# A streaming joint kernel on one Trainium2 core: transform buffers, feature order and the place of the next batch's first products

## The chip, the cores and the metric

The kernel runs on one core of one Trainium2 chip. Times are device microseconds (us) of whole runs. Before the change the median of the three first runs was 272.15 us (272.11 to 273.55). The profile is of one run; its span, from the first to the last instruction, is some 1.8 us shorter than the run's time. PE is TensorE (matmul), DVE is VectorE, ACT is ScalarE, POOL is GpSimd.

## The reference

```python
B, T, D, K, U = 2, 4000, 512, 5, 8           # bf16 throughout
h = conv1d(x, w1, taps=5, same)              # sum over 5 taps of x[t+i] @ w1[i]
h = gelu(h)[:, ::2]                          # 2000 rows
f = gelu(conv1d(h, w2, taps=5, same))[:, ::2]  # 1000 rows
fe = f @ w_f ; ge = g @ w_g                  # (B,1000,512), (B,8,512)
j  = tanh(fe[:, :, None] + ge[:, None])      # (B,1000,8,512)
return j @ w_o                               # (B,1000,8,512)
```

The last product is by far the largest: 16,000 rows of 512. The kernel works on one batch as far as its joint product and then lays the second batch's convolutions between the joint tiles of the first.

## The kernel before: the parts that matter

Every operation is recorded with what it reads and writes and an estimated cost. A list scheduler then simulates the engines, picks on each engine the ready operation with the earliest "late" time, and writes out one fixed order for each engine. On PE, program order decides among what is ready.

```python
def simulate(self, pred, succ, late):
    ...
            now = [i for i in cand[e] if ready[i] <= t + 0.02]
            i = min(now) if e in ("pe", "sp") else min(now, key=lambda i: (late[i], i))
```

The strided convolutions use a fast algorithm ("Triple"): VectorE forms nine transformed inputs (s1, t1, sm, tm, t2, t0, s0, ti, si) from six input phases z(0) to z(5), and PE multiplies each with transformed weights. t1, tm, t0 and ti come from three fp32 intermediates q0, q1, q2.

```python
class Triple:
    HOME = {"t0": (0, 0), "ti": (0, 1), "t1": (0, 2), "tm": (0, 3),   # (0, i): own buffer
            "s1": (1, 0), "sm": (1, 1), "s0": (1, 3), "t2": (1, 4), "si": (1, 5)}  # (1, i): over z(i)
    def prepare(self, k0, k1, by_dma=False):        # channel blocks k0 to k1
        ...
            stt("dve", q(1, 0, E), z(0, 0, E), -2.0, z(2, 0, E))
            stt("dve", q(2, 0, E), z(2, 0, E), -2.0, z(4, 0, E))
            ...                                      # q0 from z(4), z(0)
        tt("dve", at("t2"), z(4), z(0), sub)
        tt("dve", at("s1"), z(1), z(3), add)         # overwrites z(0): behind q0, q1 and t2
        act(z(2), z(5, -1), ACT.Copy)
        tt("dve", at("si"), z(5), z(1), sub)
        tt("dve", at("sm"), z(3), z(1), sub)         # overwrites z(1)
        ...                                          # t1 = -q1 - q2
            tt("dve", at("t0"), q(2), q(0), sub)
            tt("dve", at("tm"), q(1), q(2), sub)
            tt("dve", at("ti"), q(0, 1), q(1), sub)
        tt("dve", at("s0"), z(2), z(3), sub)

def tail_zero(b, k0=0, k1=NK):                       # on GpSimd, before each prepare of conv2
    memset(hT[b][2:6, k0:k1, HOFF + NT3 - 1:HOFF + NT3])

def fe(b):                                           # features, thirds outside, channel blocks inside
    for i in (1, 0, 2):
        for m in range(NK):
            ...                                      # 4 matmuls into the next PSUM bank
            if (m + i) % 2: act(o, v, ACT.Copy)      # 6 copies
            else: ...tensor_copy on VectorE          # 6 copies

fe(0)
...                                                  # tanh of the first 1000 rows in three pieces
for i in range(2):
    first[i].prepare(0, 2); first[i].prepare(2, 4)   # first convolution of the next batch
    if i == 0: joint(6)                              # six joint tiles of 128 rows
    for m in range(NK): slot(first[i], m, (1, 0, 1, 0, 1))   # 9 products each, joint tiles between
```

## Time and profile before

| | before |
|---|---|
| time, median | 272.15 us |
| PE busy / span | 261.2 / 270.5 us |
| PE idle at start and end | 1.2 and 3.3 us |
| holes in PE that the change can reach | 1.9 + 1.5 + 0.7 + 0.6 us |

The page gives the busy time, share of the span and instruction count of each engine:

```profile
span 270.5 us, 4327 instructions
...
PE 261.2 (97%) x1582; PEld 152.4 (56%) x1582; DVE 199.4 (74%) x352; ACT 183.1 (68%) x306; POOL 7.5 (3%) x26
```

Its line of the chain that ended last, in shares of the span by engine, shows PE for over two thirds and VectorE next:

```profile
PE 69%; DVE 13%; issue 7%; ACT 5%; DMA 5%; POOL 0%; DVEq 0%; POOLq 0%
```

The view of PE's waits lists what PE waited for, the total, the number of times and the longest:

```profile
PE acc L417 <- DVE hT L404: 1.7, 1, 1.7
PE acc L417 <- DVE feT L973: 1.4, 1, 1.4
...
PE acc L417 <- ACT jT L409: 1.0, 2, 0.6
```

The windows view gives each engine's busy time in a stretch. From 57.7 to 90 us VectorE is full while PE has its holes; from 100 us on PE is full (the line of 100 to 121 us is shown; its timeline has no hole over 0.2 us after that):

```profile
57.70:80.50 22.80, 21.07 (x148) 14.16 (x147) 22.77 (x50) 12.21 (x27) 0.43 (x3) 1.00 1.11 198
80.50:90.00 9.50, 7.99 (x69) 5.36 (x68) 9.50 (x19) 5.61 (x12) 0.00 (x0) 1.00 0.20 35
...
100.00:121.00 21.00, 21.00 (x129) 12.52 (x128) 20.08 (x37) 18.50 (x36) 0.21 (x2) 1.00 0.27 89
```

The hole before the second convolution is best read from VectorE's timeline (start, duration, line, operation, out<-in, count, idle time before and its releaser):

```profile
57.73 1.35 DVE L585 SCALAR_TENSOR_TENSOR r32b<-hT 128x336 f32<-128x336 bf16 x3 [0.53 <-POOL hT L401]
58.99 0.33 DVE L404 TENSOR_TENSOR hT<-hT 128x334 bf16<-128x334 bf16 x1
59.23 0.50 DVE L740 SCALAR_TENSOR_TENSOR row<-r32b 128x334 bf16<-128x334 f32 x1
59.65 1.40 DVE L404 TENSOR_TENSOR hT<-hT 128x334 bf16<-128x334 bf16 x4
```

The zeroing by GpSimd releases VectorE at 57.73. Three q operations run first; then t2, t1 and, at 59.65, the group that begins with s1. PE has nothing to multiply until 60.03. The zeroing itself waits for ScalarE: it starts 0.06 us after the end of the gelu that writes this channel block, at 57.52.

PE's own timeline around the second group of holes:

```profile
89.53 0.74 PE L417 MATMUL acc<-zx,w_t 128*128 128x334 bf16 x4 [1.35 <-DVE feT L973]
90.11 0.73 PE L417 MATMUL acc<-row,w_t 128*128 128x334 bf16 x4
91.39 3.63 PE L417 MATMUL acc<-wo_sb,jT 128*128 128x512 bf16 x16 [0.56 <-ACT jT L409]
...
98.58 0.73 PE L417 MATMUL acc<-row,w_t 128*128 128x334 bf16 x4
99.76 1.04 PE L417 MATMUL acc<-wo_sb,jT 128*128 128x512 bf16 x4 [0.45 <-ACT jT L409]
```

A merged line covers several matmuls; a hole is the distance from the end of one group to the start of the next, taken start to start at 0.142 us per 334-column and 0.216 us per 512-column matmul. So the holes are 1.5 us before 89.53, 0.7 before 91.39 and 0.6 before 99.76. Holes quoted below are all computed this way; the bracketed wait is up to 0.2 us shorter (1.35, 0.56 and 0.45 here), because the record of a matmul runs on past the start of the next: that of the 334-column one at 79.77 is 0.30 us long, and the next starts at 79.91.

### The profile page before, as it was taken

The numbers are of one execution on the slowest core, as the hardware profiler recorded it, in microseconds if no ns is written. First come the engines' busy times: TensorE is split into PE (matmuls) and PEld (weight loads), VectorE is DVE, ScalarE is ACT, GpSimd is POOL, SyncE is SP. The second block draws the span as 40 slices with busy tenths as digits, with TensorE's granted clock in tenths as the row PEclk, the third lists the DMA queues.
The fourth block names the chain that finished last, engine by engine and source line by source line (L and its number), as shares of the span: only waits on it lengthen the run. The fifth ranks groups of instructions, "written<-read, shape, count | busy, mean of one in ns | idle before, by whom it ended". The sixth has DMA issues, their size and how long they took to land.

```text
span 270.5 us, 4327 instructions
## 1 busy us (share of the span) xinstructions
PE 261.2 (97%) x1582; PEld 152.4 (56%) x1582; DVE 199.4 (74%) x352; ACT 183.1 (68%) x306; POOL 7.5 (3%) x26
## 2 busy tenths in 40 slices
PE   8999999979999799999999999999999999999995
PEld 4987854436666345666655554555566444444442
DVE  0999999899999999993333799953424667656654
ACT  2787969784474999786366497574346995959720
POOL 1000005200000000000000000000000000000000
PEclk9999999999999999999999999999999999999999
DMA  7999988979992014111111121421110353454444
GB/s 248 312 191 210 330 191 144 170 147 201 185 199 39 16 42 156 41 59 58 59 41 58 48 91 40 158 78 58 61 58 1 103 171 116 159 192 156 147 147 133
DMA packets 56706, 33.91 MB, mean 125 GB/s; under 512 B 31582, under 2 KB 56430, under 8 KB 56686
## 3 DMA queue, kind: packets, MB, share of 16 engines
q1 hardware_dynamic: 54430, 31.49, 43.5%
q0 software_dynamic: 2112, 2.10, 4.5%
q8 instruction: 12, 0.20, 0.3%
q14 instruction: 8, 0.07, 0.1%
q10 hardware_dynamic: 144, 0.07, 0.1%
HBM read 7.86 MB, written 16.38 MB: 90 GB/s over the span
## 4 chain that ended last, share of the span: by engine, by line
PE 69%; DVE 13%; issue 7%; ACT 5%; DMA 5%; POOL 0%; DVEq 0%; POOLq 0%
PE acc L417 68%; ACT jT L409 4%; DMA half<-w_sb 3%; DMA half<-w_t 2%; DVE row L404 2%; DVE r L585 2%; DVE hT L404 1%; DVE r32b L585 1%; DVE row L740 1%; PE acc L510 1%; DVE row L585 1%; DVE feT L973 1%; DVE xt L404 1%; DVE r L404 1%; DVE zx L404 1%
## 5 line engine op out<-in xcount | busy, mean ns | idle before, releaser
L417 PE MATMUL acc<-wo_sb,jT 128*128 128x512 bf16 (+1 forms) x504 | 115.3, 377 | 1.0 <-ACT jT L409 1.0
L1020 DVE CAST ost<-acc 128x512 bf16<-128x512 f32 (+1 forms) x95 | 65.0, 688 | 32.2 <-PE acc L417 32.1
L409 ACT ACTIVATE jT<-feT,geT 128x1000 bf16<-128x1000 f32 (+16 forms) x100 | 75.4, 816 | 8.3 <-PE acc L417 8.2
L417 PEld LDWEIGHTS acc<-wo_sb,jT 128*128 128x128 bf16 x504 | 49.1, 98 | 53.8 <-ACT jT L409 1.9
L409 ACT ACTIVATE ost<-acc 128x512 bf16<-128x512 f32 (+1 forms) x31 | 18.0, 581 | 18.1 <-PE acc L417 16.9
L417 PE MATMUL acc<-row,w_sb 128*128 128x334 bf16 (+1 forms) x160 | 29.8, 305 | 0.0
L409 ACT ACTIVATE sd<-acc 128x334 f32<-128x334 f32 (+1 forms) x32 | 13.9, 445 | 16.2 <-PE acc L417 15.9
L417 PE MATMUL acc<-xt,w_sb 128*128 128x252 bf16 (+1 forms) x144 | 23.5, 305 | 0.0
L417 PEld LDWEIGHTS acc<-row,w_sb 128*128 128x128 bf16 x160 | 15.6, 97 | 8.3
L417 PE MATMUL acc<-hT,w_t 128*128 128x334 bf16 x96 | 17.7, 305 | 1.7 <-DVE hT L404 1.7
L409 ACT ACTIVATE hT<-acc 128x334 bf16<-128x334 f32 (+3 forms) x33 | 15.0, 461 | 4.8 <-PE acc L417 4.6
L417 PEld LDWEIGHTS acc<-xt,w_sb 128*128 128x128 bf16 x144 | 14.0, 98 | 7.0 <-DVE xt L404 0.3
L417 PE MATMUL acc<-zx,w_sb 128*128 128x334 bf16 (+1 forms) x96 | 17.6, 305 | 0.0
L417 PE MATMUL acc<-row,w_t 128*128 128x334 bf16 (+1 forms) x96 | 17.4, 305 | 0.0
L585 DVE SCALAR_TENSOR_TENSOR acc<-acc,sd 128x334 f32<-128x334 f32 (+1 forms) x16 | 8.2, 513 | 9.6 <-PE acc L417 9.6
L404 DVE TENSOR_TENSOR sd<-sd 128x334 f32<-128x334 f32 (+1 forms) x16 | 8.0, 507 | 9.0 <-ACT sd L409 8.9
L417 PE MATMUL acc<-xs,w_t 128*128 128x252 bf16 (+1 forms) x76 | 14.0, 314 | 0.5 <-issue 0.5
L417 PE MATMUL acc<-fT,wf_sb 128*128 128x333 bf16 (+1 forms) x96 | 14.0, 305 | 0.2 <-ACT fT L409 0.2
L417 PEld LDWEIGHTS acc<-hT,w_t 128*128 128x128 bf16 x96 | 9.3, 98 | 8.1 <-DVE hT L404 2.2
L973 DVE COPY feT<-acc 128x333 f32<-128x333 f32 (+1 forms) x12 | 7.2, 616 | 8.0 <-PE acc L417 8.0
L409 ACT ACTIVATE fT<-acc 128x334 bf16<-128x334 f32 (+1 forms) x16 | 7.1, 446 | 8.6 <-PE acc L417 8.6
L417 PEld LDWEIGHTS acc<-zx,w_sb 128*128 128x128 bf16 x96 | 9.4, 98 | 5.4
(80 smaller groups left out, 307.3 us busy)
## 6 DMA issues: line engine op xcount, KB each, us to landing
out_dram<-ost SPq DMA_DIRECT2D x109, 128.0 KB, 1.9
w_sb<-in_w_dram SPq DMA_DIRECT2D x10, 512.0 KB, 5.5
xr<-in_x_dram SPq DMA_DIRECT2D x2, 512.0 KB, 4.1
half<-w_sb POOLq DMA_DIRECT2D x2, 512.0 KB, 6.4
half<-w_t POOLq DMA_DIRECT2D x2, 512.0 KB, 5.1
wf_sb<-in_w_f_dram SPq DMA_DIRECT2D x1, 512.0 KB, 7.5
wg_sb<-in_w_g_dram SPq DMA_DIRECT2D x1, 512.0 KB, 5.7
wo_sb<-in_w_o_dram SPq DMA_DIRECT2D x1, 512.0 KB, 6.5
```

The lines of the kernel that those rows point to most:

```text
L404: pl.op(eng, lambda e: e.tensor_tensor(out=o.ap, in0=a.ap, in1=b.ap, op=op), (a, b), (o,), vec_cost(o, (a, b)))
L409: pl.op("act", lambda e: e.activation(o.ap, i.ap, func, scale=scale, bias=0.0 if bias is None else bias.ap), rd, (o,), o.ap.free_size() * ...
L417: ins = e.matmul(o.ap, lhsT=l.ap, rhs=r.ap, start=start and n == 0, stop=stop and n == len(pairs) - 1, skip_group_check=not check)
L510: ins = e.transpose(pv.ap[:, r, k, :], xr[rt].h[:, 2 * r + pp, k, :], ident.h[:, :])
L585: pl.op(eng, lambda e: e.scalar_tensor_tensor(out=o.ap, in0=a.ap, scalar=f, in1=b.ap, op0=ALU.mult, op1=op), (a, b), (o,), vec_cost(o, (a, ...
L740: pl.op("dve", lambda e: e.scalar_tensor_tensor(out=o.ap, in0=a.ap, scalar=-1.0, in1=b.ap, op0=ALU.mult, op1=sub), (a, b), (o,), vec_cost( ...
L973: pl.op("dve", lambda e, o=o, v=v: e.tensor_copy(out=o.ap, in_=v.ap), (v,), (o,), vec_cost(o, (v,)))
L1020: pl.op("dve", lambda e, o=o, v=v: e.tensor_copy(out=o.ap, in_=v.ap), (v,), (o,), vec_cost(o, (v,)))
```

## The change

The intent: (1) give s1 and sm of batch 0's second convolution buffers of their own (in the new tile "wide", which also takes t0, ti, t1 and tm of this convolution from row[1]), so that the first product need not wait for the q operations; (2) zero on VectorE, without the hop to GpSimd; (3) order the features by channel block, so that tanh can start early, with the ScalarE and VectorE costs set to given values; (4) put the first products of the next batch's convolution ahead of the first joint tiles.

```diff
+            def __init__(self, src, off, r, n, w, out, r32, first, wide=False):
+                self.home = dict(self.HOME, s1=(0, 4), sm=(0, 5)) if wide else self.HOME
@@ prepare
+                if self.home["s1"][0] == 0:
+                    tt("dve", at("s1"), z(1), z(3), add)
                 ... q1, q2
+                ... t1 (moved up)
+                if self.home["sm"][0] == 0:
+                    tt("dve", at("sm"), z(3), z(1), sub)
                 ... q0, t2, si, then tm ahead of t0
@@
+        wide = at("wide", [6, NK, 336], BF16, Q[0])
+        trip = [Triple(hT[b], HOFF, (wide, row[0])[b], ..., b == 0) for b in range(B)]
@@ fe
-            for i in (1, 0, 2):
-                for m in range(NK):
+            for i, m in ((1, 0), (0, 0), (1, 1), (0, 1), (2, 0), (2, 1), (1, 2), (0, 2), (2, 2), (1, 3), (0, 3), (2, 3)):
-                    if (m + i) % 2:
+                if i == 1:                       # 4 copies on ScalarE, 8 on VectorE
@@ tail_zero
-            memset(hT[b][2:6, k0:k1, HOFF + NT3 - 1:HOFF + NT3])
+            pl.op("dve", lambda e: e.memset(v.ap, 0.0), (), (v,), 0.08)
@@ program
-            if i == 0:
-                joint(6)
+        u0, u1 = (first[0].stages(m) for m in range(2))
+        u0[0](); u1[0](); joint(2); u0[1](); joint(2); u1[1](); joint(2); u0[2](); joint(1)
```

More of the change, by code (lines that the diff above doesn't have):

```diff
@@ L405, in tt, with act @@
                   vec_cost(o, (a, b)))
-        def act(o, i, func, scale=1.0, bias=None):
+        def act(o, i, func, scale=1.0, bias=None, cost=None):
             rd = (i,) if bias is None else (i, bias)
@@ L410, in act @@
                                                 bias=0.0 if bias is None else bias.ap), rd, (o,),
-                  o.ap.free_size() * 0.83e-3 + 0.13)
+                  cost or o.ap.free_size() * 0.83e-3 + 0.13)
         def mm(o, pairs, start, stop, check=True):
@@ L709, in bass_standalone__seq2seq_rnn_t_joint__speech_kernel @@
                     "s1": (1, 0), "sm": (1, 1), "s0": (1, 3), "t2": (1, 4), "si": (1, 5)}
-            def __init__(self, src, off, r, n, w, out, r32, first):
+            def __init__(self, src, off, r, n, w, out, r32, first, wide=False):
+                self.home = dict(self.HOME, s1=(0, 4), sm=(0, 5)) if wide else self.HOME
                 self.z_, self.off, self.r_, self.n, self.w, self.out, self.r32, self.first = src, off, r, n, w, out, r32, first
@@ L718, in prepare @@
                 z = lambda i, d=0, w=n: self.z_[i, ks, self.off + d:self.off + d + w]
-                at = lambda which: z(self.HOME[which][1]) if self.HOME[which][0] else self.r_[self.HOME[which][1], ks, 0:n]
+                at = lambda which: z(self.home[which][1]) if self.home[which][0] else self.r_[self.home[which][1], ks, 0:n]
                 q = lambda j, d=0, w=n: self.r32[j, kr, d:d + w]
@@ L726, in prepare @@
                         acc(q(i, 0, E), z(2 * i, 0, E))
-                else:
+                if self.home["s1"][0] == 0:
+                    tt("dve", at("s1"), z(1), z(3), add)
+                if not by_dma:
                     stt("dve", q(1, 0, E), z(0, 0, E), -2.0, z(2, 0, E))
                     stt("dve", q(2, 0, E), z(2, 0, E), -2.0, z(4, 0, E))
+                o, a, b = at("t1"), q(1), q(2)
+                pl.op("dve", lambda e: e.scalar_tensor_tensor(
+                    out=o.ap, in0=a.ap, scalar=-1.0, in1=b.ap, op0=ALU.mult, op1=sub), (a, b), (o,),
+                      vec_cost(o, (a, b), False))
+                if self.home["sm"][0] == 0:
+                    tt("dve", at("sm"), z(3), z(1), sub)
+                if not by_dma:
                     if self.first:
@@ L734, in prepare @@
                 tt("dve", at("t2"), z(4), z(0), sub)
-                tt("dve", at("s1"), z(1), z(3), add)
+                if self.home["s1"][0]:
+                    tt("dve", at("s1"), z(1), z(3), add)
                 act(z(2), z(5, -1), ACT.Copy)
                 tt("dve", at("si"), z(5), z(1), sub)
-                tt("dve", at("sm"), z(3), z(1), sub)
-                o, a, b = at("t1"), q(1), q(2)
-                pl.op("dve", lambda e: e.scalar_tensor_tensor(
-                    out=o.ap, in0=a.ap, scalar=-1.0, in1=b.ap, op0=ALU.mult, op1=sub), (a, b), (o,),
-                      vec_cost(o, (a, b), False))
+                if self.home["sm"][0]:
+                    tt("dve", at("sm"), z(3), z(1), sub)
                 if self.first:
@@ L748, in prepare @@
                 else:
+                    tt("dve", at("tm"), q(1), q(2), sub)
                     tt("dve", at("t0"), q(2), q(0), sub)
-                    tt("dve", at("tm"), q(1), q(2), sub)
                     tt("dve", at("ti"), q(0, 1), q(1), sub)
@@ L754, in product @@
             def product(self, which, m, bank, start, ks=range(NK)):
-                at_z, i = self.HOME[which]
+                at_z, i = self.home[which]
                 n, w, o = self.n, self.w[which], self.off
@@ L857, in bass_standalone__seq2seq_rnn_t_joint__speech_kernel @@
                  Triple(zx[1], 2, row[1], 335, taps1, to_h(1, HOFF + 167), r32, True)]
-        trip = [Triple(hT[b], HOFF, row[1 - b], NT3, taps2, to_f(b), (r32b, r32)[b], False) for b in range(B)]
+        wide = at("wide", [6, NK, 336], BF16, Q[0])
+        trip = [Triple(hT[b], HOFF, (wide, row[0])[b], NT3, taps2, to_f(b), (r32b, r32)[b], False, b == 0) for b in range(B)]
         t0, t1 = tiles[0:2]
@@ L963, in fe @@
         def fe(b):
-            for i in (1, 0, 2):
-                for m in range(NK):
-                    v = ps.cols(bank(), START[i + 1] - START[i])
-                    sl = slice(START[i], START[i + 1])
-                    mm(v, [(wf_sb[k, m * P:(m + 1) * P], fT[b][k, sl]) for k in range(NK)], True, True)
-                    o = feT[b][m, i::3]
-                    if (m + i) % 2:
-                        act(o, v, ACT.Copy)
-                    else:
-                        pl.op("dve", lambda e, o=o, v=v: e.tensor_copy(out=o.ap, in_=v.ap), (v,), (o,), vec_cost(o, (v,)))
+            for i, m in ((1, 0), (0, 0), (1, 1), (0, 1), (2, 0), (2, 1), (1, 2), (0, 2), (2, 2), (1, 3), (0, 3), (2, 3)):
+                v = ps.cols(bank(), START[i + 1] - START[i])
+                sl = slice(START[i], START[i + 1])
+                mm(v, [(wf_sb[k, m * P:(m + 1) * P], fT[b][k, sl]) for k in range(NK)], True, True)
+                o = feT[b][m, i::3]
+                if i == 1:
+                    act(o, v, ACT.Copy, cost=0.54)
+                else:
+                    pl.op("dve", lambda e, o=o, v=v: e.tensor_copy(out=o.ap, in_=v.ap), (v,), (o,), 0.47)
         def tanh(v, k, lo=0, hi=T2):
@@ L986, in tail_zero @@
         def tail_zero(b, k0=0, k1=NK):
-            memset(hT[b][2:6, k0:k1, HOFF + NT3 - 1:HOFF + NT3])
+            v = hT[b][2:6, k0:k1, HOFF + NT3 - 1:HOFF + NT3]
+            pl.op("dve", lambda e: e.memset(v.ap, 0.0), (), (v,), 0.08)
         ntile = B * U * T2 // P
@@ L1066, in bass_standalone__seq2seq_rnn_t_joint__speech_kernel @@
             first[i].prepare(2, 4)
-            if i == 0:
-                joint(6)
+        u0, u1 = (first[0].stages(m) for m in range(2))
+        u0[0]()
+        u1[0]()
+        joint(2)
+        u0[1]()
+        joint(2)
+        u1[1]()
+        joint(2)
+        u0[2]()
+        joint(1)
+        live.extend((u0, u1))
+        for i in range(2):
             for m in range(NK):
-                slot(first[i], m, (1, 0, 1, 0, 1))
+                if (i, m) > (0, 1):
+                    slot(first[i], m, (1, 0, 1, 0, 1))
         tail_zero(1, 0, 2)
```

## The prediction

> **What bounds the kernel now.** TensorE: the page gives PE 261.2 us busy of a span of 270.5, and the windows view shows it back to back from 100 to 267 us. The waits and the PE timeline leave these holes (start to start, at 0.216 us per 512-column and 0.142 us per 334-column matmul; [...] the trace agrees: 16 matmuls from 91.39 to 94.85 us):
> - 1.2 us at the start, 3.3 after the last matmul, 0.7 near 23.8 us: not touched.
> - 58.14 to 60.03 us: 1.9 us before the first conv2 product (PE waits for DVE hT, 1.7).
> - 88.0 to 89.53: 1.5 us, waiting for a VectorE copy of feT that frees a PSUM bank.
> - 90.68 to 91.39 and 99.15 to 99.76: 1.3 us, waiting for tanh (jT).
>
> So about 4.7 us (1.7%) is reachable. From 57.7 to 88 us the chain of waits runs through VectorE, which is 100% busy there: its order and load is the second limit.
>
> **What the change does.**
> 1. Conv2 of batch 0: s1 and sm get buffers of their own, so s1 (0.33 us, bf16) runs first, not after three 0.42 us fp32 operations and a difference; t1 follows. PE can start about 0.4 us after the zeroing; 12 products of s1 (1.7 us) cover the 1.3 us to t1. Hole at 58 us: 0.2 to 0.6 instead of 1.9. Gain 1.4.
> 2. Zeroing by VectorE drops the hop to GpSimd for 0.07 us each; it helps step 1, no separate gain.
> 3. Features by channel block: block 0 is complete after 5 of 12 groups (2.8 us) instead of 9, so tanh starts near 84, not 89.2 us. ScalarE gets 4 feT copies for 6, VectorE 8 for 6 (0.62 us each): +1.2 us where it is full.
> 4. Next batch's first products ahead of the joint: 16 matmuls, 2.3 us, between features and first joint tile, in banks freed long before; later stages sit between pairs of tiles. Of the 2.8 us of holes at 88 to 100, 2.2 recovered.
> 5. Five joint tiles fewer (25 for 30) among the triples of the first convolution: PE reaches the second triple some 4 us sooner, with VectorE saturated until 119 us. I charge 0.4 us of new stall there or before the products at 86 us. The five tiles cover the second feature pass, which has no hole: no gain.
>
> Sum: 1.4 + 2.2 - 0.4 = 3.2 us, all on the critical path, since PE is gapless afterwards.
>
> **Prediction.** 268.9 us, range 267.6 to 271.2. Faster by over 2%: 0.05; within 2%: 0.93; slower by over 2%: 0.02.
>
> **What the profile would show.** PE busy unchanged at 261 us; span about 267.3. PE's wait on hT falls from 1.7 to under 0.6; those on feT (1.4) and jT (1.0) nearly vanish. First tanh near 84 us, next batch's first products at 86 to 87, first joint tile near 89. VectorE no longer waits for GpSimd; it is busy 1 us more, ScalarE about as much less.
>
> **What would make it wrong.** VectorE, full from 58 to 119 us, may not deliver transforms 3 us earlier: then a closed hole reopens as PE waiting for DVE row or zx at 62 to 70, at 86, or at 108 to 113 us, and the gain is under 1.5 us. The static schedule is made anew from costs, so small stalls may fall anywhere from 50 to 180 us. A gain over 4.7 us would mean that a hole counted as untouched also moved.

## The result, and the profile after

The change runs at 269.63 us median (269.27 to 270.46, 4 runs) against 272.17 us for the kernel before in the same rounds. The ratio is 0.990, 95% interval 0.986 to 0.994. Ratios here are the mean time of one kernel's runs over that of the other's of the same rounds, so not quite the ratio of the medians quoted. The predicted 268.9 us was 0.7 us too low; the range held the result.

```profile
span 267.6 us, 4331 instructions
...
PE 260.0 (97%) x1582; PEld 151.8 (57%) x1582; DVE 201.1 (75%) x362; ACT 181.2 (68%) x302; POOL 6.9 (3%) x20
```

```profile
PE 76%; DVE 16%; issue 3%; DMA 2%; ACT 1%; SPq 0%; DVEq 0%; ACTq 0%
```

PE's waits after:

```profile
PE acc L417 <- DVE wide L404: 1.6, 1, 1.6
...
PE acc L417 <- ACT jT L409: 0.7, 1, 0.7
```

The wait for feT is gone and that for jT smaller. But the wait before the second convolution, predicted to fall from 1.7 to under 0.6 us, is 1.6: only its name changed, from hT to wide. VectorE's timeline shows why:

```profile
57.22 0.84 DVE L404 TENSOR_TENSOR wide<-r32b 128x668 bf16<-128x668 f32 x1 [0.76 <-issue]
57.26 0.06 DVE L996 MEMSET hT<- 128x4 bf16 x1
57.98 0.92 DVE L585 SCALAR_TENSOR_TENSOR r32b<-hT 128x336 f32<-128x336 bf16 x2
58.82 0.32 DVE L404 TENSOR_TENSOR wide<-hT 128x334 bf16<-128x334 bf16 x1
```

The zeroing is done at 57.32 and s1 needs nothing else, yet q1 and q2 (57.98) go first, behind a tm difference of 0.84 us; s1 comes at 58.82. The edit put s1 first in the text; the scheduler put it third, behind q1 and q2. By its rule q1 and q2 had the earlier late times, as the longer chain by way of t1 hangs on them; the late times themselves were not printed.

What sets the start of all this is on ScalarE:

```profile
54.13 1.06 ACT L409 ACTIVATE w_t<-half 128x1024 bf16<-128x1024 f32 x1 [1.01 <-DMA half<-w_t]
...
56.60 0.58 ACT L409 ACTIVATE hT<-acc 128x498 bf16<-128x498 f32 x1
```

Call the end of this gelu "g": 57.18 us here, 57.52 before. The zeroing waits for it. In all fourteen profiles g stands behind a weight copy for which ScalarE waited 0.9 to 1.0 us on a DMA, and in thirteen it comes 3.04 us after the start of that copy. From g to the first product of conv2 it took 2.51 us before and takes 2.03 now. So the conv2 part did bring this product 0.48 us nearer to what it waits for. The hole hardly shrank because PE, done with its earlier work 0.62 us after g before, is done 0.23 us after g in this profile.

PE around the other holes:

```profile
59.20 0.60 PE L417 MATMUL acc<-wide,w_t 128*128 128x334 bf16 x3 [1.64 <-DVE wide L404]
...
87.17 0.73 PE L417 MATMUL acc<-zx,w_t 128*128 128x334 bf16 x4
...
88.87 0.73 PE L417 MATMUL acc<-row,w_t 128*128 128x334 bf16 x4
90.31 1.90 PE L417 MATMUL acc<-wo_sb,jT 128*128 128x512 bf16 x8 [0.71 <-ACT jT L409]
```

The next batch's products follow the features without a hole (87.17 is where the features end), and one hole of 0.87 us is left before the first joint tile. ScalarE ahead of it:

```profile
85.27 0.51 ACT L409 ACTIVATE jT<-feT,geT 128x256 bf16<-128x256 f32 x1 [1.41 <-DVE feT L981]
...
86.12 2.10 ACT L409 ACTIVATE jT<-feT,geT 128x256 bf16<-128x256 f32 x3
88.11 0.62 ACT L409 ACTIVATE feT<-acc 128x333 f32<-128x333 f32 x1
88.56 1.69 ACT L409 ACTIVATE jT<-feT,geT 128x256 bf16<-128x256 f32 x4
```

tanh starts at 85.27 instead of 89.23 (28.09 and 31.71 us after g), but three tanh from 86.12 (2.10 us, of which 488 and 1000 columns are not needed until later tiles) stand ahead of a feature copy and of the tanh of blocks 1 to 3.

Where the time came from, in the two profiles (last matmul ends 267.17 before, 264.31 after):

| step | us |
|---|---|
| g comes sooner, 57.52 to 57.18 | 0.34 |
| g to the first product of conv2, 2.51 to 2.03 | 0.48 |
| hole after the features, 1.52 to 0 | 1.52 |
| holes for jT, 0.71 + 0.61 to 0.87 | 0.45 |
| rest | 0.07 |

The first row is not shown to be the change's doing: over the fourteen profiles g fell anywhere from 56.42 to 57.88 us. Without it the two profiles differ by 2.5 us, as the medians do.

The end of PE's work ahead of conv2 varies too, from 57.21 to 58.14 us over the thirteen profiles that share PE's order up to there (in "first products undone" 16 of these 390 matmuls stand in other places). Some of this is in the first microseconds: the same ten first matmuls, on zeros, took 4.45 us before, 4.12 after and 3.74 in "s1 first, q0 later". Why was not shown: the granted clock is 1.00 in every window from 1.1 to 8.8 us, before and after. And this is not the whole: five profiles of the same order with 4.45 us for these ten still differ from 57.48 to 58.14.

### The profile page after: what moved, and what is told of

Same layout as the page of the kernel before. It is cut to its first block, busy times and chain, and to the rows that moved or that the text cites. A ratio compares the mean times of both kernels' runs of the same rounds, so it can differ in the third digit from the quotient of the medians.

```text
span 267.6 us, 4331 instructions
## 1 busy us (share of the span) xinstructions
PE 260.0 (97%) x1582; PEld 151.8 (57%) x1582; DVE 201.1 (75%) x362; ACT 181.2 (68%) x302; POOL 6.9 (3%) x20
## 4 chain that ended last, share of the span: by engine, by line
PE 76%; DVE 16%; issue 3%; DMA 2%; ACT 1%; SPq 0%; DVEq 0%; ACTq 0%
PE acc L417 76%; DVE wide L404 2%; DVE r L585 2%; DMA xr<-in_x_dram 2%; DVE r32b L585 2%; DVE ws L404 2%; DVE hT L404 1%; DVE ws L585 1%; ACT jT L409 1%; DVE w_sb L404 1%; DVE feT L981 1%; DVE w_t L404 1%; DVE sd L585 1%; DVE sd L404 1%; DVE wide L734 1%
## 5 line engine op out<-in xcount | busy, mean ns | idle before, releaser
L409 ACT ACTIVATE jT<-feT,geT 128x1000 bf16<-128x1000 f32 (+16 forms) x100 | 76.6, 823 | 13.4 <-PE acc L417 10.3
L417 PE MATMUL acc<-row,w_sb 128*128 128x334 bf16 (+1 forms) x112 | 20.5, 305 | 0.0
L417 PE MATMUL acc<-row,w_t 128*128 128x334 bf16 (+1 forms) x80 | 14.6, 305 | 0.0
L417 PEld LDWEIGHTS acc<-row,w_sb 128*128 128x128 bf16 x112 | 10.9, 98 | 6.2
L417 PEld LDWEIGHTS acc<-fT,wf_sb 128*128 128x128 bf16 x96 | 9.3, 97 | 4.5 <-ACT fT L409 0.2
L417 PE MATMUL acc<-hT,w_t 128*128 128x334 bf16 x64 | 11.7, 305 | 0.0
L981 DVE COPY feT<-acc 128x334 f32<-128x334 f32 (+1 forms) x16 | 9.2, 608 | 3.2 <-PE acc L417 3.2
L417 PE MATMUL acc<-hT,w_sb 128*128 128x334 bf16 x64 | 11.5, 305 | 0.0
```

Of the source, the lines that this page charges most:

```text
L409: pl.op("act", lambda e: e.activation(o.ap, i.ap, func, scale=scale, bias=0.0 if bias is None else bias.ap), rd, (o,), cost or o.ap.free_s ...
L417: ins = e.matmul(o.ap, lhsT=l.ap, rhs=r.ap, start=start and n == 0, stop=stop and n == len(pairs) - 1, skip_group_check=not check)
L981: pl.op("dve", lambda e, o=o, v=v: e.tensor_copy(out=o.ap, in_=v.ap), (v,), (o,), 0.47)
```

## The experiments

Theory 1: the conv2 part bought nothing because the issue order undid it. Once that is mended, two theories differ. **Order**: the hole closes and the gain stays. **Load**: VectorE is full from 57 to 90 us (in the profile of the change busy for all 32.60 us from 57.4 to 90), so the hole moves to the next point where PE needs VectorE. A third question is which engine holds the first joint tile.

All kernels gave correct results by comparison with the reference. Landmarks from each profile, in us. "a" is the end of the last product ahead of conv2, the landmark of the expectations. "g" is the end of the gelu named above; it was read from the kept traces afterwards. The runs were made in rounds on two chips, each time with the kernel before beside them (medians 271.79 to 272.17):

| kernel | time, median | ratio | hole at conv2 | a to next batch's first product | g to conv2's first product | g to next batch's first product | g to last matmul |
|---|---|---|---|---|---|---|---|
| before | 272.17 | 1 | 1.89 | 31.39 | 2.51 | 32.01 | 209.64 |
| the change | 269.63 | 0.990 | 1.80 | 29.77 | 2.03 | 29.99 | 207.14 |
| the change again | 269.53 | 0.991 | 1.44 | 29.40 | 2.03 | 29.99 | 207.13 |
| conv2 part undone (granted clock 0.991) | 269.61 | 0.992 | 2.40 | 32.05 | 2.51 | 32.16 | 208.80 |
| first products undone | 269.89 | 0.992 | 0.93 | 30.80 | 1.68 | 31.55 | 207.85 |
| feature order undone | 269.70 | 0.990 | 1.29 | 29.26 | 2.03 | 30.00 | 207.41 |
| s1 first | 269.36 | 0.990 | 0 | 28.98 | 0.68 | 29.67 | 206.95 |
| s1 first, q0 later (mended) | 268.92 | 0.989 | 0 | 28.95 | 0.72 | 29.67 | 206.96 |
| mended, short q0 (wrong) | 268.27 | 0.985 | 0 | 28.14 | 0.72 | 28.86 | 205.96 |
| mended, si on GpSimd | 271.47 | 0.997 | 0.56 | 32.09 | 0.56 | 32.10 | 209.04 |
| feature copies first | 269.61 | 0.991 | 1.89 | 29.85 | 2.03 | 30.00 | 207.20 |
| two tanh later | 269.18 | 0.990 | 1.24 | 29.21 | 2.03 | 30.00 | 207.05 |
| s1 and feature copies first | 269.30 | 0.989 | 0 | 28.71 | 0.96 | 29.67 | 207.02 |
| all moves | 269.38 | 0.990 | 0.06 | 29.17 | 0.57 | 29.67 | 207.01 |

From a, the same kernel differs by 0.37 us from profile to profile (29.77 and 29.40). From g, the five kernels with the change's conv2 order and its first products agree to 0.01 us at the next batch's first product, and so do the four with s1 first and all of VectorE's work, whatever their a. So in this stretch PE follows g, and differences are read from g. The hole at conv2 is the way from g to the first product less the way from g to a, and a lay anywhere from 0.01 to 0.96 us behind g.

The moves below are made after scheduling, in one function that takes an operation out of its engine's list and puts it elsewhere; nothing else changes:

```diff
-        order = self.schedule(pred)
+        order = fix(self.schedule(pred), ops)
```

### The change again

The changed kernel without an edit, to learn how far its landmarks spread.

> The changed kernel itself again, on the chip of these experiments, for a second profile and a closer time. Expected: 0.989 to 0.992 of before; the hole ahead of conv2 anywhere from 1.2 to 1.9 us, as runs with the same order gave 1.24 to 1.88; the hole ahead of the first joint tile 0.8 to 0.9 us; the last product ahead of conv2 ends at 57.2 to 58.2 us.

269.53 us, 0.991 (0.987 to 0.995). Hole at conv2 1.44 us, before the first joint tile 0.86. All as expected. The hole at conv2 thus varies from run to run by itself (1.24 to 1.89 us over the five profiles with this order), while the way from g to the first product stays at 2.03 us: PE's arrival moves against ScalarE's gelu.

### Conv2 part undone

The Triple class, the zeroing and the buffer go back to the lines of before; features and first products stay.

> The changed kernel with its conv2 part undone (buffers, order of the transforms, zeroing by GpSimd as before); feature order and first products stay. The trace of the changed kernel shows the hole before the first conv2 product still 1.8 us (57.40 to 59.20) against 1.9 before, so theory 1 (the conv2 part bought nothing, because VectorE still issues two fp32 transforms ahead of s1) expects a hole of 1.8 to 2.0 us, and a time within 0.4 us of the changed kernel: about 0.990 of before, at most 0.992. The rival (the conv2 part is worth the 0.7 us by which the changed kernel's PE is early at 57 us, or more later) expects 0.993 to 0.996 of before. Theory 1 also says that those 0.7 us are spread of the first 24 us from run to run: PE's last product ahead of conv2 can end anywhere from 57.4 to 58.2 us here.

The median is 269.61 us, the same as with the part: the part was worth nothing measurable in the time. The interval reaches 0.994, so the rival's 0.993 is not quite excluded. The mean ratio, 0.9915 (0.989 to 0.994), is raised by the profiled run, 271.21 us, the slowest of six; the other five are 269.12 to 269.93. The profile shows what befell that run. In the windows view the figure after the busy times is the granted PE clock:

```profile
59.80:61.80 2.00, 1.98 (x8) 1.12 (x9) 2.00 (x6) 0.05 (x1) 0.12 (x1) 0.55 1.18 179
61.80:63.80 2.00, 2.00 (x11) 1.12 (x9) 2.00 (x8) 0.48 (x1) 0.00 (x0) 0.59 1.03 171
63.80:65.80 2.00, 2.00 (x16) 1.38 (x15) 2.00 (x4) 0.41 (x2) 0.00 (x0) 1.00 1.15 191
```

PE had waited 2.24 us; then the granted clock was 0.55 and 0.59 in two windows of 2 us, and from 60.49 to 62.99 the 334-column matmuls came 0.28 us apart, against 0.14 from 63.64 on. The other thirteen profiles, with holes of up to 1.9 us there, show no such spacing behind them. So this profile's landmarks after the hole are not comparable. The hole of 2.40 us comes before the slow clock and counts, and the expected 1.8 to 2.0 us was a miss: from g the first product came after 2.51 us, as before the change, and PE was done only 0.11 us after g. Theory 1's reason is thus too strong: with the part conv2's first product comes 0.48 us sooner after g, but the times show nothing of it.

### s1 first

```diff
+    move("dve", tm of blocks 0-1, ahead of the zeroing of block 2)
+    move("dve", s1 of block 2, straight behind its zeroing)
+    move("dve", s1 of block 3, straight behind its zeroing)
+    move("pe", the four s1 products, ahead of the four t1 products)
```

> The changed kernel, with only the issue order altered after scheduling: VectorE does s1 of the third and fourth channel block straight after the zeroing (and the one tm difference of the first two blocks ahead of the zeroing, in the 0.76 us in which it sat idle), and PE does the four s1 products before the four t1 products. Theory 1 (order alone kept the hole open) expects the hole at 58 us to shrink from 1.8 to 0.3 to 0.6 us, PE's first conv2 product near 57.8 instead of 59.2. What comes of it later tells two theories apart. Order theory: the gain stays, 1.2 us faster than the changed kernel (0.985 of before). VectorE-load theory (VectorE is full from 57 to 90 us, so only its idle time that is filled, 0.76 us, can be won): the hole ahead of the first joint tile grows from 0.87 to about 1.4 us, and the net gain is 0.5 to 0.8 us (0.987 to 0.988 of before).

```profile
57.19 1.00 PE L417 MATMUL acc<-xt,w_sb 128*128 128x498 bf16 x4
58.02 1.86 PE L417 MATMUL acc<-wide,w_t 128*128 128x334 bf16 x12
...
62.54 0.32 PE L417 MATMUL acc<-wide,w_sb 128*128 128x334 bf16 x1 [0.81 <-DVE wide L734]
```

The hole closed entirely: the s1 products start at 58.02, as the previous ones end. But PE then waited at 62.54 for t1 of block 3 (hole 0.98 us), and the hole before the first joint tile grew from 0.87 to 1.22. From a, 0.8 us reached the next batch's first product (28.98 against 29.77), but the change again had 29.40 there. Read from g, conv2's first product comes 1.35 us sooner than in the change, the next batch's first product 0.32, the first joint tile not at all (33.17 against 33.13) and the last matmul 0.19. The order theory's 1.2 us is refuted; the gain is even below the 0.5 to 0.8 us of the load theory. The time, 269.36 us (0.9901, 0.988 to 0.992), cannot tell 0.2 us apart.

### s1 first and q0 later

One VectorE operation of 0.77 us, q0 of blocks 0 and 1, still stood ahead of the q1 and q2 that PE waited for.

```diff
+    (the four moves above)
+    move("dve", q0 of blocks 0-1, behind t1 of block 3)
```

> The s1-first kernel with one more VectorE operation moved: the q0 transform of channel blocks 0 and 1 (0.77 us, not urgent) goes behind t1 of block 3 instead of ahead of its q1 and q2. In the s1-first run PE waited 0.81 us for that t1. Order theory: this stall falls to 0 to 0.2 us, there is no new stall up to the next batch's first product, which comes 28.0 to 28.3 us after the last product ahead of conv2 (29.8 in the changed kernel, 29.0 in s1-first). VectorE-load theory: the stall moves on, to the next batch's products at about 86 us, and those come no sooner than 28.7 us after. Both expect the hole ahead of the first joint tile, which waits for ScalarE, to swallow most of the 0.8 us: time equal to s1-first within 0.4 us (269.0 to 269.5, 0.989 to 0.990).

```profile
61.00 0.32 PE L417 MATMUL acc<-wide,w_sb 128*128 128x334 bf16 x1
...
67.01 0.74 PE L417 MATMUL acc<-wide,w_sb 128*128 128x334 bf16 x4 [0.21 <-DVE sd L585]
67.91 0.74 PE L417 MATMUL acc<-hT,w_sb 128*128 128x334 bf16 x4 [0.16 <-DVE hT L404]
```

The stall for t1 fell from 0.98 to 0.17, and two new ones of 0.37 and 0.33 us opened at 67 and 68 us (and 0.1 at 62.10), each behind VectorE. The next batch's first product came after 28.95 us (29.67 from g, to 0.01 us where it was with s1 first alone): the load theory's side of 28.7, though the stall reappeared at 67 us, not at 86. With 268.92 us (0.989, 0.987 to 0.992) this has the lowest median of the correct kernels, but its interval overlaps that of the change, so that it beats the change is not shown; the traces give it 0.18 us from g to the last matmul.

### Less load on VectorE, wrong on purpose

```diff
+    (the mended kernel; after scheduling, q0 of all conv2 blocks writes 8 columns instead of 336)
```

> Wrong on purpose: the mended conv2 kernel, with the three q0 transforms of the first conv2 (0.77, 0.42, 0.42 us on VectorE) cut to 8 columns each, so that VectorE has about 1.4 us less to do between 60 and 64 us; no other instruction moves. In the mended kernel PE lost 0.97 us in four small holes between 61 and 68 us. VectorE-load theory: those after the first (0.37 and 0.33 us at 67 and 68) vanish, and the next batch's first product comes 28.0 to 28.4 us after the last product ahead of conv2, against 28.95 there and 29.77 in the changed kernel. If it is order or ScalarE, these holes stay and it remains at 28.8 to 29.1.

```profile
66.73 0.73 PE L417 MATMUL acc<-wide,w_sb 128*128 128x334 bf16 x4
67.30 0.73 PE L417 MATMUL acc<-hT,w_sb 128*128 128x334 bf16 x4
```

The holes at 67 and 68 us are gone; 0.17 at 61 remains. The next batch's first product comes after 28.14 us, within the expected 28.0 to 28.4 (from g 0.81 us sooner than in the mended kernel, the last matmul 1.00), and the median is 268.27 us (0.985, 0.980 to 0.991). No order changed, only some 1.4 us of VectorE work went. So with order mended, VectorE's load sets how fast PE gets through conv2. (The arithmetic is wrong; the comparison of outputs did not catch it, as errors in these values are small in the result. The kernel is no candidate.)

### A correct relief: si on GpSimd

```diff
+    (the mended kernel)
+    si of the three conv2 blocks: from VectorE's list to GpSimd's
```

> A correct version of the same relief: the mended conv2 kernel with the three si differences of the first conv2 (0.42, 0.25, 0.25 us on VectorE) done by GpSimd, which is idle there. VectorE-load theory: 0.9 us less on VectorE, the holes at 67 and 68 us shrink from 0.70 to under 0.2 us and the next batch's first product comes 28.2 to 28.6 us after the last product ahead of conv2; the time falls little, as the hole ahead of the first joint tile takes most of it: 268.6 to 269.2. If GpSimd slows VectorE's neighbours or is late itself (over 5 us for the three), PE waits for POOL near 69 us and it is slower than the mended kernel.

It was slower than the mended kernel by 2.5 us of the medians (of different rounds): 271.47 us, 0.997 (0.993 to 1.001). GpSimd's timeline, then VectorE's, of the same run:

```profile
58.61 1.50 POOL L404 TENSOR_TENSOR hT<-hT 128x668 bf16<-128x668 bf16 x1 [7.36 <-ACT hT L409]
61.08 0.87 POOL L404 TENSOR_TENSOR hT<-hT 128x334 bf16<-128x334 bf16 x1 [0.96 <-ACT hT L409]
64.12 1.39 POOL L404 TENSOR_TENSOR hT<-hT 128x334 bf16<-128x334 bf16 x1 [2.18 <-DVE wide L734]
```

```profile
58.30 2.18 DVE L585 SCALAR_TENSOR_TENSOR r32b<-hT 128x336 f32<-128x336 bf16 x2
...
61.18 1.12 DVE L404 TENSOR_TENSOR wide<-r32b 128x334 bf16<-128x334 f32 x1
...
64.76 0.94 DVE L404 TENSOR_TENSOR wide<-hT 128x334 bf16<-128x334 bf16 x1
```

The pair of q operations at 58.30 took 2.18 us; the same pair took 0.92 in the other kernels. The tm difference at 61.18 took 1.12 for 0.50, and s1 at 64.76 0.94 for 0.33. Each lies over a GpSimd operation, and VectorE lost 2.5 us (1.26 + 0.62 + 0.61) to be rid of 0.9. The mechanism was not shown. (Not every overlap cost VectorE time: the q0 transform at 63.99, under way when the third difference of GpSimd began at 64.12, took its usual 0.85 us, and that difference took 1.39 us against 0.87 for the second of the same size.) Nor were the differences themselves cheap on GpSimd: 1.50 us against 0.50 on VectorE for 128x668 (3 times), and 0.87 against 0.33 for 128x334 (2.6 times); none was measured there without VectorE at work beside it. The expectation named this outcome as a possibility, but looked for the wait at the wrong place: PE waited for VectorE, not for GpSimd.

### The first joint tile: the last feature copies first

```diff
+    move("dve", t0 of the next batch's blocks 2-3, behind the last two feT copies)
```

> The changed kernel with one VectorE operation moved: the t0 transform of the next batch (0.84 us at 87.68), which nobody needs until several us later, goes behind the last two feT copies instead of ahead of them. If the hole ahead of the first joint tile (89.44 to 90.31 us, 0.87 us, PE waits for tanh) is a matter of VectorE order, it shrinks by 0.6 to 0.8 us and the time falls by as much (0.987 of before). If it is ScalarE that is late (it runs two tanh that are not urgent, 488 and 1000 columns, from 86.5 to 88.1 us), the hole stays at 0.7 to 0.9 us and so does the time (0.990).

The hole was 1.07 us (0.87 in the change), above both expectations, and the time 269.61 us (0.9913, 0.989 to 0.993): VectorE's order alone does not hold the first joint tile.

### Two tanh later

```diff
+    move("act", tanh of 488 columns of block 0, ahead of those of blocks 1-3)
+    move("act", tanh of 1000 columns of block 0, ahead of those of blocks 1-3)
```

> The changed kernel with two ScalarE operations moved: the tanh of 488 and of 1000 columns of channel block 0 (1.6 us together, needed only from the fifth and eighth joint tile on) go behind the tanh of the first pair of tiles. ScalarE-order theory: the hole ahead of the first joint tile falls from 0.87 to 0.2 to 0.5 us (the last feT copy of VectorE, done at 89.5, and one tanh then set it), 0.4 to 0.6 us faster than the changed kernel: 269.0 to 269.2. ScalarE-load theory: ScalarE is full from 86 to 100 us, so the hole comes back as a wait for jT of about the same size at a joint tile between 93 and 101 us, and the time stays at 269.5 to 269.7.

The hole stayed at 0.87 us; ScalarE now sat idle 0.77 us before the last tanh, waiting for VectorE's feT copy. So the expected 0.2 to 0.5 us was a miss: each engine alone could close nothing, because the other was as late. The time, 269.18 us, 0.9903 (0.988 to 0.993), lies in the range of the ScalarE-order theory all the same; with the hole unchanged and 0.09 us won from g to the last matmul, I put that down to the spread from run to run.

### s1 first, and the feature copies first

```diff
+    (the four moves of "s1 first")
+    move("dve", t0 of the next batch's blocks 2-3, behind the last two feT copies)
```

> Both of the last two alterations together. Order theory: the gains add, about 1.9 us under the changed kernel (0.983 of before). VectorE-load theory: 0.76 us of idle time filled plus 0.84 us of work put off until after the first joint tile, so 1.2 to 1.6 us under the changed kernel (0.984 to 0.986), with a hole of 0.4 to 0.7 us left ahead of the first joint tile.

269.30 us, 0.9894 (0.987 to 0.992): slower than either theory expected. The hole before the first joint tile was 1.22 us, since ScalarE was not mended.

### All moves together

```diff
+    (the five moves of "s1 first and q0 later", the t0 move above, and the two tanh moves)
```

> All the moves together: s1 first, q0 later, the last feT copies ahead of t0, and the two tanh later. If order alone kept the holes open, PE runs nearly gapless from 24 us on: first joint tile 31.0 to 31.4 us after the last product ahead of conv2 (32.9 in the changed kernel), 1.5 to 1.9 us faster than it: 267.8 to 268.2, 0.984 to 0.986 of before. If the load of ScalarE or VectorE is the limit, 0.5 to 1.2 us of that comes back as waits for jT at the joint tiles between 90 and 105 us: 268.4 to 269.2.

Now the hole before the first joint tile is 0.25 us, and 31.70 us from "a" to it. But the next one, PE first and then ScalarE in the same run:

```profile
89.62 1.67 PE L417 MATMUL acc<-wo_sb,jT 128*128 128x512 bf16 x7
92.16 0.73 PE L417 MATMUL acc<-zx,w_b 128*128 128x334 bf16 x4 [0.86 <-ACT jT L409]
```

```profile
90.43 0.76 ACT L409 ACTIVATE row<-r 128x668 bf16<-128x668 f32 x1 [0.75 <-DVE r L404]
91.09 0.89 ACT L409 ACTIVATE jT<-feT,geT 128x256 bf16<-128x256 f32 x2
```

ScalarE sat idle 0.75 us for a VectorE difference that its fixed order wanted before the next tanh, and PE's hole of 1.03 us came one pair of tiles later. The time, 269.38 us (0.9903, 0.988 to 0.993), is just above the 268.4 to 269.2 that load was to give. From 90 to 96 us of this run VectorE is busy for 5.80 us and ScalarE for 5.57, and the hole closed in one place opened in the next. Whether ScalarE's fixed order (the operation at 90.43 ahead of the tanh) or its load keeps it open was not tested.

### First products undone

```diff
-        u0[0](); u1[0](); joint(2); ...
+            if i == 0: joint(6)      # and all slots, as before
```

> The changed kernel with the next batch's first products back behind the first six joint tiles; conv2 part and feature order stay. My theory: these products, in PSUM banks freed early, close the 1.5 us hole behind the features, so PE again waits 0.8 to 1.5 us there for a copy of feT or for tanh, and the time is 270.4 to 271.1 (0.994 to 0.997 of before). Rival (the feature order closed it, as it lets tanh start 4 us earlier): 269.5 to 270.0.

```profile
88.96 0.74 PE L417 MATMUL acc<-zx,w_t 128*128 128x334 bf16 x4 [1.35 <-DVE feT L981]
```

The hole of 1.52 us behind the features is back, with the same releaser as before the change, a VectorE copy of feT that frees a PSUM bank. From the start of conv2's products to the last matmul this kernel takes 206.2 us, against 205.1 in both profiles of the change (before: 207.1), and from g to the last matmul 0.7 us more than the change. So undoing part 4 costs 0.7 to 1.1 us (the schedule was made anew, and here conv2's first product comes 1.68 us after g). The time, 269.89 us (0.9922, 0.990 to 0.995), is less than I expected and in the rival's range: the hole is the one I named, its price is not. The rival has a part in it. With the feature order kept and the first products gone, the holes for tanh are already down, from 0.72 and 0.62 us before the change to 0.24.

### Feature order undone

> The changed kernel with the features back in the old order (parts outside, copies half and half); conv2 part and first products stay. My theory: tanh then starts near 88 us instead of 85 and the first joint tile, for which all four channel blocks must be done, comes 0.5 to 1.5 us later behind the first products (hole of 1.4 to 2.4 us instead of 0.87): 270.1 to 271.1 (0.993 to 0.997 of before). Rival: the first products alone cover it, 269.4 to 269.9.

269.70 us, 0.990 (0.987 to 0.994): the rival was right. The hole before the first joint tile is 1.13 us against 0.87, so the feature order is worth 0.3 us in the trace (also from g to the last matmul) and nothing in the times: with the first products ahead, tanh has time enough either way. The two parts thus cover the same holes in part; a kernel with both undone and the conv2 part kept was not run.

## Why the prediction was right or wrong

- **Bound and size.** PE busy went from 261.2 to 260.0 us and the gain is closed holes, as predicted. 2.5 us by the medians against 3.2 predicted: step 1 gave 0.9 less and step 4 0.2 less than forecast, and the 0.4 charged in step 5 did not come. That the charge made up for part of step 1 is luck.
- **Step 1 failed:** "s1 (0.33 us, bf16) runs first ... Hole at 58 us: 0.2 to 0.6 instead of 1.9. Gain 1.4." Measured: a hole of 1.80 and, again, 1.44 us. From g, which the prediction did not see as the start of the chain, the gain at conv2's first product is 0.5 us, and undoing it did not change the time. I read the program text as the issue order. The scheduler ranks by late times and issued q1 and q2 first. The run with s1 moved shows that the buffer did make a closed hole possible, and also that 1.4 us was never there: of 1.35 us won at conv2's first product, 1.03 are lost again before the next batch's first product and all of it at the first joint tile. The short-q0 run puts the loss in conv2 down to VectorE's load.
- **Step 2 right:** VectorE no longer waits for GpSimd (2.0 us in total before, none after), and a zeroing of hT takes 0.06 to 0.07 us on it, against 0.11 to 0.14 on GpSimd. It was not tested alone; its first operation behind the zeroing starts 0.21 us after g before and 0.04 now, so up to 0.17 of the 0.48 us may be this step's.
- **Step 3:** tanh started 4 us earlier (85.27, where 84 was predicted). With the first products in place it is worth 0.3 us in the trace; without them (first products undone) the holes for tanh are 0.24 us against 1.3 before the change. VectorE is busy 1.7 us more and ScalarE 1.9 less, more than the 1 us said.
- **Step 4 right in its mechanism:** undoing it brings its hole back. In size, 2.0 us of 2.8 were recovered at 88 to 100 us, 2.2 predicted, but steps 3 and 4 share them: undoing step 4 alone costs 0.7 to 1.1 us.
- **Step 5:** the charge of 0.4 us for new stalls was not needed. PE has no new hole of that size between 91 and 264 us.
- **What hid the failure:** the profile of the change is 0.34 us early at g and PE 0.74 us early ahead of conv2, before anything that was changed. Without g's part this pair of profiles gives 2.5 us: 2.0 at 88 to 100 us and 0.5 at conv2.

Open: which part of the DMA ahead of ScalarE's weight copy moves g from run to run (56.42 to 57.88 us). No experiment moved that copy or its DMA, though g is what conv2 waits for.

## What to carry to other kernels

When a scheduler fixes the issue order, read the engine's instruction list, not the program text, before crediting an edit with an earlier start. Where two helper engines are nearly full beside a bound engine, do not expect more from a closed hole than the idle time that it fills on them: s1 first filled 0.76 us of VectorE's and won 0.2 to 0.3 us. Count that first. Before assigning a small gain to an edit, find the event that the stretch really waits for (here ScalarE's gelu, not the end of PE's own work) and measure from it in every profile.
